# Feature projections of a Performer attention as native float32 products of 64 rows on the two halves of TensorE, with paced attention steps

## The chip, the cores and the metric

The kernel runs on one core of one Trainium2 chip. The metric is the device time of one execution in microseconds (us), as the median of several runs. A profile is one further execution, recorded by the hardware profiler. The engines are called as the profile calls them: PE is TensorE's matmul, PEld its weight load, DVE is VectorE, ACT is ScalarE, POOL is GpSimd, SP is the queue that issues the DMAs.

## The reference

A linear attention with random features is followed by two dense layers with gates, all in float32:

```python
batch, n_heads, seq, head_dim, n_features = 4, 8, 576, 64, 128
def phi(x):
    proj = np.einsum('bhsd,md->bhsm', x, omega)
    sq = np.sum(x * x, axis=-1, keepdims=True) / 2.0
    h = proj - sq
    h = h - np.max(h, axis=-1, keepdims=True)
    return np.exp(h) / np.sqrt(m)
q_p, k_p = (phi(q_s), phi(k_s))               # q_s = q * scale, k_s = k * scale
kv = np.einsum('bhsm,bhsd->bhmd', k_p, v)
num = np.einsum('bhsm,bhmd->bhsd', q_p, kv)
den = np.einsum('bhsm,bhm->bhs', q_p, k_p.sum(2))[..., None] + 1e-06
# x = (num / den) as 2304 tokens of 512, then
# layer 0: h = x @ w_in (512 -> 2048); g = h * clip(h + 3, 0, 6) / 6; x = g @ w_out
# layer 1: h = x @ w_in;               g = h * sigmoid(1.702 h);      out = g @ w_out
```

The term `sq` falls out, since the row's maximum is subtracted after it.

## The kernel before

**Tiling.** Of the 576 rows of a sequence, 512 are worked as four tiles of 128; the 64 left over of all heads go through their own tiles (`lqk`, `lv`, `el`). The work runs in blocks: the dense layers handle one batch (512 tokens) per block, 16 chunks of 128 hidden units each, layer 0 for batches 0 to 3, then layer 1 for batches 0 to 3. The last block of each layer also carries the 256 left-over tokens. The attention of batch 0 stands ahead of everything (the prologue, until 58.5 us in the profiled execution). The attention of batch n+1 is woven into block n of layer 0, so blocks 0, 1 and 2 carry attention, block 3 and layer 1 none. The first product of `emit_h` (line 439) in the blocks 1, 2, 3 and 4 starts at 183.7, 310.0, 438.8 and 570.0 us.

**Products in three parts.** A float32 product is made of three single-pass float32r products, with each operand split into a high part and a rest: hi·hi + hi·lo + lo·hi. This holds for the dense layers (`emit_h`, line 439, and `emit_o`, line 501, twelve products of 512 columns per chunk each) and for the feature projections. For these, `T` copies queries and keys of one head to float32r (`thi`, line 266) and subtracts (`tlo`, line 267), both on DVE; `TL` does the same with the left-over rows. The stationary operand of `project` (line 225) holds 64 dimensions of two row tiles in its 128 rows, and the moving operand `bd_hi`, `bd_lo` is omega twice, block by block with zeros, 256 columns. So one `PJ(h, j)` is two groups of three products of 256 columns, with j = 0 for keys and j = 1 for queries, and one bank of PSUM.

**The other steps of a head.** `features` takes the row maxima on DVE (`mx`, line 231) and four exponentials on ACT (line 233). `KV` (lines 292 and 300) multiplies feature keys with values in native float32, as pairs of products that write two halves of 64 PSUM partitions; ACT copies `kv` (line 308). `QT` (line 315) transposes the feature queries, ACT copies `qpt` (line 317). `NU` (lines 329 and 338) multiplies `qpt` with `kv`, DVE normalizes into `xt` (lines 351 to 356). `XT` (line 367) transposes a finished pair of heads, ACT and DVE split it into `x` (lines 219 and 220), which `emit_h` reads.

**Weights.** Each of the 32 chunks of weights is loaded raw and converted (`convert_w`): ACT makes `wtop` and `w` (lines 186, 187), DVE three bit operations (189 to 197), POOL two multiplications (202), DVE two additions (205), ACT casts (210), POOL subtractions (211). Layer 0's sixteen chunks are converted up to the end of block 0, layer 1's in blocks 1 to 3. Ten of the 32 half chunks of a layer stay in SBUF (`HELD`), the others are fetched again for each block.

**What sets the order.** `att_steps` lists an attention's 57 steps. In the prologue they follow one another, and the first conversion is put 12 steps before the end (`TAIL`). In a block, `side` runs one step at each of its four calls per chunk (two in `emit_h`, two in `emit_o`) until none are left. PSUM banks in a block come from four rotating buffers (`ps`), shared by `emit_h` and all attention steps. A scheduler moves instructions within each engine's list when the program is built; the lists are then fixed.

## Time and profile before

| | |
|---|---|
| runs | 984.83 us median of 3 (983.9 to 987.41) |
| profiled execution | 987.94 us, of which 986.0 us are the span |
| PE busy | 950.1 us (96%), 5626 products |
| PEld busy | 788.6 us (80%) |
| DVE busy | 470.3 us (48%) |
| ACT busy | 416.9 us (42%) |
| POOL busy | 196.3 us (20%) |
| mean granted clock of TensorE | 0.988 |

The busy time of a product includes the time in which it drains while the next one already streams, so a busy PE is not a PE at its peak. The distance between the starts of products tells what they cost. Busy shares over the whole span mix the stretch with attention and conversions (until 570 us) with the stretch of dense layers alone. The chain of waits, followed back from the last instruction, names at each step what released it.

### The profile page before, as it was taken

What the parts mean: (1) busy time and instruction counts of PE and PEld (TensorE: products, weight loads), DVE (VectorE), ACT (ScalarE), POOL (GpSimd) and SP (SyncE); (2) the same over time, 40 slices, a digit from 0 to 9 for tenths busy, and PEclk for the clock granted to TensorE, in tenths of its full rate; (3) what the DMA queues carried; (4) which work ended last, traced back from release to release, by engine and by line L of the source; (5) the groups of instructions that cost most, each with busy time, mean ns of one, the idle gap of its engine ahead of it and who ended that gap; (6) DMA issues with size and microseconds to landing.
All of it is one profiled execution on the core that took longest, in us unless ns stands there. A gap on an engine that the chain in (4) does not pass through costs nothing.

```text
span 986.0 us, 14412 instructions
## 1 busy us (share of the span) xinstructions
PE 950.1 (96%) x5626; PEld 788.6 (80%) x5626; DVE 470.3 (48%) x813; ACT 416.9 (42%) x868; POOL 196.3 (20%) x159
## 2 busy tenths in 40 slices
PE   8899999999989999999999999999999999999994
PEld 7777776888768877878888888888888888888883
DVE  7888887886776876324222232222223222322221
ACT  5876777666655664433222232132223222312221
POOL 0346565534433342021000011020002000000000
PEclk9899999999999999999999999999999999999998
DMA  6676577987787875246333374436335333422301
GB/s 197 234 262 200 199 264 251 345 298 260 269 293 260 305 249 174 74 147 214 124 121 122 126 256 149 147 130 214 128 128 192 129 128 128 137 77 86 107 1 64
DMA packets 54774, 177.22 MB, mean 180 GB/s; under 512 B 5812, under 2 KB 7476, under 8 KB 54708
## 3 DMA queue, kind: packets, MB, share of 16 engines
q1 hardware_dynamic: 54708, 176.32, 52.5%
q8 instruction: 44, 0.72, 0.3%
q14 instruction: 22, 0.18, 0.1%
HBM read 138.55 MB, written 37.75 MB: 179 GB/s over the span
## 4 chain that ended last, share of the span: by engine, by line
PE 64%; DVE 12%; DMA 7%; ACT 6%; POOL 5%; issue 3%; SPq 0%; POOLq 0%; ACTq 0%
PE ps L439 30%; PE o L501 30%; DMA ws1i<-wsn 4%; DVE w L205 4%; POOL wsn L211 3%; POOL w L202 2%; DMA ws1o<-wsn 2%; ACT wtop L186 1%; DVE gs L460 1%; DVE mx L231 1%; DVE wmag L189 1%; ACT w L187 1%; PE ps L225 1%; DVE wtop L193 1%; ACT e L233 1%
## 5 line engine op out<-in xcount | busy, mean ns | idle before, releaser
L439 PE MATMUL ps<-x,wss 128*128 128x512 f32 x1152 | 286.3, 393 | 7.7 <-ACT wss L210 6.1
L439 PEld LDWEIGHTS ps<-x,wss 128*128 128x128 f32 x1152 | 212.0, 188 | 53.0 <-ACT wss L210 7.0
L457 DVE TENSOR_TENSOR ga<-ga,ps 128x512 f32<-128x512 f32 x80 | 50.8, 635 | 252.4 <-ACT ga L456 252.4
L456 ACT ACTIVATE ga<-ps 128x512 f32<-128x512 f32 x80 | 44.4, 556 | 251.7 <-PE ps L439 251.7
L501 PE MATMUL o<-gs,wss 128*128 128x512 f32 (+1 forms) x600 | 136.8, 375 | 0.0
L460 DVE TENSOR_TENSOR gs<-ga,gs 128x512 fp32r<-128x512 f32 (+1 forms) x160 | 111.4, 712 | 47.2 <-ACT gs L459 44.2
L501 PE MATMUL o<-wss,gs 128*128 128x512 f32 x540 | 129.8, 389 | 0.0
L501 PEld LDWEIGHTS o<-wss,gs 128*128 128x128 f32 x540 | 100.7, 188 | 20.5
L501 PEld LDWEIGHTS o<-gs,wss 128*128 128x128 f32 x600 | 102.5, 189 | 17.9
L459 ACT CAST gs<-ga 128x512 fp32r<-128x512 f32 (+1 forms) x160 | 91.7, 578 | 44.1 <-DVE ga L457 32.5
L452 DVE SCALAR_TENSOR_TENSOR ga<-ga,ps 128x512 f32<-128x512 f32 x80 | 50.2, 629 | 111.2 <-ACT ga L451 111.2
L439 PE MATMUL ps<-x,wsh 128*128 128x512 f32 x384 | 95.6, 393 | 1.5 <-ACT wsh L210 0.8
L202 POOL TENSOR_TENSOR w<-w,wpow 128x512 f32<-128x512 f32 x64 | 77.3, 1229 | 94.5 <-DVE wpow L197 70.4
L451 ACT ACTIVATE ga<-ps,three 128x512 f32<-128x512 f32 x80 | 51.8, 651 | 94.9 <-PE ps L439 94.7
L501 PE MATMUL o<-gs,wsh 128*128 128x512 f32 (+1 forms) x360 | 86.1, 383 | 0.3 <-DVE gs L460 0.3
L439 PEld LDWEIGHTS ps<-x,wsh 128*128 128x128 f32 x384 | 70.9, 188 | 16.7 <-ACT wsh L210 1.3
L205 DVE TENSOR_TENSOR w<-w,wtop 128x512 f32<-128x512 f32 x64 | 73.4, 1163 | 16.8 <-POOL w L202 16.6
L501 PE MATMUL o<-wsh,gs 128*128 128x512 f32 x324 | 78.5, 389 | 0.0
L541 POOL TENSOR_TENSOR x<-xr,x 128x512 fp32r<-128x512 f32 x16 | 22.2, 1417 | 263.8 <-ACT x L540 263.8
L233 ACT ACTIVATE e<-ps,mx 128x128 f32<-128x128 f32 x220 | 63.7, 387 | 25.3 <-DVE mx L231 25.2
L501 PEld LDWEIGHTS o<-gs,wsh 128*128 128x128 f32 x360 | 64.1, 195 | 12.6 <-DVE gs L460 0.7
L501 PEld LDWEIGHTS o<-wsh,gs 128*128 128x128 f32 x324 | 60.4, 188 | 12.3
(123 smaller groups left out, 1003.8 us busy)
## 6 DMA issues: line engine op xcount, KB each, us to landing
wss<-ws1i SPq DMA_DIRECT2D x48, 512.0 KB, 3.2
wss<-ws1o SPq DMA_DIRECT2D x40, 512.0 KB, 3.3
wss<-ws0i SPq DMA_DIRECT2D x36, 512.0 KB, 4.4
wraw<-in_w_in_dram SPq DMA_DIRECT2D x32, 512.0 KB, 4.5
wraw<-in_w_out_dram SPq DMA_DIRECT2D x32, 512.0 KB, 6.0
wss<-ws0o SPq DMA_DIRECT2D x30, 512.0 KB, 3.5
ws1i<-wsn SPq DMA_DIRECT2D x16, 512.0 KB, 3.8
ws1o<-wsn SPq DMA_DIRECT2D x16, 512.0 KB, 2.9
```

Of the source, the lines that this page charges most:

```text
L202: nc.gpsimd.tensor_tensor(out=w[:, cols], in0=w[:, cols], in1=q[:, cols], op=ALU.mult)
L205: nc.vector.tensor_tensor(out=wj, in0=wj, in1=a[:, j * DM:(j + 1) * DM], op=ALU.add)
L211: nc.gpsimd.tensor_tensor(out=s[:, 1], in0=wj, in1=s[:, 0].bitcast(F32), op=ALU.subtract)
L233: act = nc.scalar.activation(out=e[:, r, :], in_=ps[:, r, :], func=AF.Exp, bias=mx[:, r:r + 1])
L439: nc.tensor.matmul(out=ps, lhsT=w[:, wi, kk, :], rhs=x[:, xi, kk, :], start=(m == 0), stop=(m == 3 * NK - 1),)
L451: nc.scalar.activation(out=g, in_=ps, func=AF.Relu, bias=three)
L452: nc.vector.scalar_tensor_tensor(out=g, in0=g, scalar=6.0, in1=ps, op0=ALU.min, op1=ALU.mult)
L456: nc.scalar.activation(out=g, in_=ps, func=AF.Sigmoid, scale=1.702)
L457: nc.vector.tensor_tensor(out=g, in0=g, in1=ps, op=ALU.mult)
L459: nc.scalar.copy(s[:, 0, :], g)
L460: nc.vector.tensor_tensor(out=s[:, 1, :], in0=g, in1=s[:, 0, :].bitcast(F32), op=ALU.subtract)
L501: last = nc.tensor.matmul(out=ps[:, e, :], lhsT=lhsT, rhs=rhs, start=(c == 0 and m == 0 and per == 1), stop=(c == NC - 1 and m == 2 and e ...
```

## The change

The split of keys, queries and left-over rows is gone, with `T`, `TL`, `bd_hi` and `bd_lo`. `project` is one native float32 product per row tile: 64 rows of the raw `qk` tile are stationary, the 128 columns of `omt` (omega times the scale) are moving. The two row tiles that shared a stationary operand before now use the lower and the upper 64 rows of the array, each with a PSUM bank of its own. `PJ(h)` covers keys and queries in one step, eight products, `PL` the left-over rows, eight products. The feature tile `e` holds keys and queries, with three buffers (`EB`). `KV` comes ahead of `QT`. The steps are 39, and `side` runs one only when the share of steps done falls behind the share of its 64 calls in a block. `HELD` goes from 10 to 11, `TAIL` from 12 to 10.

```diff
-    def project(ps, lhs_hi, lhs_lo):
-        o = ps.rearrange("p a m -> p (a m)")
-        for n, (a, w) in enumerate(((lhs_hi, bd_hi), (lhs_hi, bd_lo), (lhs_lo, bd_hi))):
-            nc.tensor.matmul(
-                out=o, lhsT=a, rhs=w.rearrange("p a m -> p (a m)"), start=(n == 0), stop=(n == 2)
-            )
+    HALVES = (slice(0, D), slice(D, 2 * D))
+
+    def project(ps, n, rows, lhsT):
+        nc.tensor.matmul(out=ps[:, n, :], lhsT=lhsT, rhs=omt[rows, :], start=True, stop=True)
...
-        def T(self, h):
...
-        def PJ(self, h, j):
-            hi, lo = self.t[h]
-            ps = bank([P, R, M], "ps")
-            for g in range(2):
-                project(ps[:, 2 * g:2 * g + 2, :], hi[:, j, g, :], lo[:, j, g, :])
-            e = at.tile([P, R, M], F32, tag=f"e{j}", bufs=2, name="e")
-            self.feat[h] = features(ps, e)
-            self.e[h, j] = e
+        def PJ(self, h):
             a = qkv[self.b, h // 2][0][:, h % 2]
+            ps = [bank([P, R, M], "ps") for _ in HALVES]
+            for j in range(2):
+                for g in range(2):
+                    for p, rows in zip(ps, HALVES):
+                        project(p, 2 * j + g, rows, a[rows, j, g, :])
+            e = at.tile([P, 2, 2, 2, M], F32, tag="e", bufs=EB, name="e")
+            for half, p in enumerate(ps):
+                self.feat[h] = features(p, e[:, half].rearrange("p j g m -> p (j g) m"))
+            self.e[h] = e
...
             if 1 <= h <= H:
+                st.append(lambda h=h: a.KV(h - 1))
                 st.append(lambda h=h: a.QT(h - 1))
-                st.append(lambda h=h: a.KV(h - 1))
...
+    pace = [0, 0]
 
     def side():
-        if todo:
+        pace[1] += 1
+        while todo and (pace[0] - len(todo)) * 4 * NC < pace[0] * pace[1]:
             todo.pop()()
```

**The projections on PE.** In the list of PE, batch 0's fourth head stood before as six products of 256 columns for the keys, with the queries' six after other work (the names are output and inputs):

```order
L225 MATMUL ps_389<-bd_hi_85,thi_332 128x256
L225 MATMUL ps_389<-bd_lo_86,thi_332 128x256
L225 MATMUL ps_389<-bd_hi_85,tlo_333 128x256
L225 MATMUL ps_389<-bd_hi_85,thi_332 128x256
L225 MATMUL ps_389<-bd_lo_86,thi_332 128x256
L225 MATMUL ps_389<-bd_hi_85,tlo_333 128x256
L329 MATMUL acc_345<-kv_302,qpt_289 64x65 x8
```

Now the same head's first products alternate between two banks, one for each half of the rows:

```order
L302 MATMUL acc_322<-ident_78,e_230 128x128 x4
L226 MATMUL ps_339<-omt_143,qk_154 128x128
L226 MATMUL acc_340<-omt_143,qk_154 128x128
L226 MATMUL ps_339<-omt_143,qk_154 128x128
L226 MATMUL acc_340<-omt_143,qk_154 128x128
```

Not every set of eight stands like this. Batch 0's fifth head has the four products of one half together, then a transposition `XT` (line 354 now), then the four of the other half:

```order
L302 MATMUL ps_396<-ident_78,e_273 128x128 x4
L226 MATMUL ps_410<-omt_143,qk_329 128x128 x4
L354 MATMUL acc_403<-ident_78,xt_294 128x128 x4
L226 MATMUL acc_411<-omt_143,qk_329 128x128 x4
L279 MATMUL acc_448<-v_155,e_349 64x65
L316 MATMUL ps_434<-kv_394,qpt_401 64x65 x8
```

Over the whole list, 23 of the 36 sets of eight products alternate (some of these with one neighbour out of place), in 6 the two halves follow as four and four, and in 7 other work stands between the two halves.

**Steps apart.** In block 1 before, between `NU` (lines 329 and 338) and the `XT` that transposes its result (line 367), PE had this:

```order
L329 MATMUL ps<-kv,qpt 64x65 x8
L338 MATMUL ps<-kv,qtl 64x65 x2
L439 MATMUL ps<-x_864,wsh 128x512 x6
L315 MATMUL ps<-ident,e 128x128 x4
L439 MATMUL ps<-x_864,wsh 128x512 x6
L292 MATMUL ps<-v,e 64x65 x8
L300 MATMUL ps<-lv,el 64x65 x2
L367 MATMUL ps<-ident,xt 128x128 x4
```

Now, at one such place in block 1 (`NU` is lines 316 and 325, `KV` 279 and 287, `QT` 302, `XT` 354, the dense layers 421 and 483):

```order
L316 MATMUL ps<-kv,qpt 64x65 x8
L325 MATMUL ps<-kv,qtl 64x65 x2
L421 MATMUL ps<-x_774,wss 128x512 x12
L279 MATMUL ps<-v,e 64x65 x8
L287 MATMUL ps<-lv,el 64x65 x2
L483 MATMUL o<-gs,wsh 128x512 x6
L302 MATMUL ps<-ident,e 128x128 x4
L483 MATMUL o<-gs,wsh 128x512 x6
L421 MATMUL ps<-x_774,wss 128x512 x6
L354 MATMUL ps<-ident,xt 128x128 x4
```

The dense products between the two steps went from 12 to 30.

**ACT at the first conversion.** In the prologue, ACT's list had the first conversion (lines 186 and 187) between the features of the fifth head and the copy of `kv`:

```order
L317 COPY qpt_521<-acc_516 128x512
L233 ACTIVATE e_490<-acc_483,mx_491 128x128 x4
L186 ACTIVATE wtop_695<-wraw_383 128x1024
L187 ACTIVATE w_698<-wraw_383 128x1024
L187 ACTIVATE w_871<-wraw_386 128x1024
L308 COPY kv_534<-ps_523 128x65
```

Now the same three stand there, ahead of `kv` and `qpt` (lines 295 and 304):

```order
L232 ACTIVATE e_420<-acc_411,mx_427 128x128 x4
L187 ACTIVATE wtop_632<-wraw_333 128x1024
L188 ACTIVATE w_635<-wraw_333 128x1024
L188 ACTIVATE w_781<-wraw_336 128x1024
L295 COPY kv_459<-acc_448 128x65
L304 COPY qpt_466<-ps_461 128x512
```

Here the place of the conversion stayed; the order of `kv` and `qpt` behind it is turned round.

## Rows read from the trace of the kernel before

**Rows 1.** The page, busy time, share of the span and instructions of each engine.

```profile
PE 950.1 (96%) x5626; PEld 788.6 (80%) x5626; DVE 470.3 (48%) x813; ACT 416.9 (42%) x868; POOL 196.3 (20%) x159
```

**Rows 2.** Busy time by stretch: prologue and blocks 0, 1, 2.

```profile
core 0: us, PE busy (x) PEld busy (x) DVE busy (x) ACT busy (x) POOL busy (x), PEclk, DMA share, GB/s
0.00:58.50 58.50, 49.55 (x511) 42.24 (x511) 46.04 (x110) 40.89 (x115) 14.78 (x19) 0.94 0.70 229
58.50:183.70 125.20, 118.95 (x807) 93.36 (x807) 106.29 (x173) 88.29 (x172) 72.30 (x56) 1.00 0.71 246
183.70:310.00 126.30, 122.91 (x841) 99.30 (x840) 93.62 (x160) 78.78 (x167) 50.12 (x39) 0.99 0.79 279
310.00:438.80 128.80, 125.67 (x854) 101.68 (x853) 75.52 (x131) 67.96 (x156) 34.04 (x28) 0.99 0.57 196
```

**Rows 3.** Chain of waits, shares of the stretch 0 to 184 us by line.

```profile
by line: DVE w L205 13.8%; POOL w L202 6.8%; PE ps L439 5.7%; DVE mx L231 5.5%; DVE wmag L189 5.4%; issue 5.1%; ACT wtop L186 4.8%; DVE gs L460 4.6%; DVE wtop L193 4.3%; ACT e L233 3.7%; PE ps L225 3.1%; DVE tlo L267 2.7%; DVE thi L266 2.5%
```

**Rows 4.** PE timeline, dense layers alone: start, us, engine, line, op, out<-in, shape, count.

```profile
640.97 2.88 PE L501 MATMUL o<-wss,gs 128*128 128x512 f32 x12
643.69 2.88 PE L439 MATMUL ps<-x,wss 128*128 128x512 f32 x12
```

**Rows 5.** PE timeline in block 2: dense products, KV and a projection's first products.

```profile
403.53 1.52 PE L439 MATMUL ps<-x,wss 128*128 128x512 f32 x6
404.98 0.69 PE L292 MATMUL ps<-v,e 128*64 128x65 f32 x16
405.60 0.33 PE L300 MATMUL ps<-lv,el 64*64 64x65 f32 x4
405.86 1.66 PE L439 MATMUL ps<-x,wss 128*128 128x512 f32 x6
407.36 0.28 PE L225 MATMUL ps<-bd_hi,thi 128*128 128x256 f32 x1
407.48 0.28 PE L225 MATMUL ps<-bd_lo,thi 128*128 128x256 f32 x1
```

**Rows 6.** PE timeline: products with 64 rows and all 128 columns of the array.

```profile
58.46 0.46 PE L374 MATMUL acc<-ident,xln 64*128 64x64 f32 x4
58.86 3.93 PE L439 MATMUL ps<-x,wss 128*128 128x512 f32 x16
```

**Rows 7.** PE timeline: NU's left-over products and KV's first ones.

```profile
22.11 0.34 PE L338 MATMUL ps<-kv,qtl 128*64 128x65 f32 x3
22.23 0.27 PE L292 MATMUL ps<-v,e 128*64 128x65 f32 x1
22.28 0.22 PE L338 MATMUL ps<-kv,qtl 128*64 128x65 f32 x1
```

**Rows 8.** Operand splits, grouped by line: busy us, mean ns, then idle before.

```profile
L267 DVE TENSOR_TENSOR tlo<-qk,thi 128x512 fp32r<-128x512 f32 x32 | 24.5, 765 | 0.1
L266 DVE CAST thi<-qk 128x512 fp32r<-128x512 f32 x32 | 18.4, 575 | 11.0 <-PE ps L225 6.5 <-DMA qk<-in_qk_dram 2.7 <-PE acc L225 1.8
```

**Rows 9.** PE timeline: four of its waits, in brackets idle us and releaser.

```profile
31.54 1.13 PE L329 MATMUL acc<-kv,qpt 128*64 128x65 f32 x16 [2.43 <-ACT kv L308]
56.66 0.73 PE L439 MATMUL ps<-x,wss 128*128 128x512 f32 x2 [2.21 <-ACT wss L210]
286.20 0.63 PE L367 MATMUL ps<-ident,xt 128*128 128x128 f32 x4 [2.57 <-DVE xln L356]
375.08 0.69 PE L292 MATMUL ps<-v,e 128*64 128x65 f32 x16 [2.24 <-DVE tlo L267]
```

**Rows 10.** Granted clock after two waits (columns as rows 2), and dense products there.

```profile
287.40:290.50 3.10, 3.10 (x9) 2.36 (x8) 1.61 (x3) 1.42 (x4) 1.28 (x1) 0.50 0.55 169
376.20:379.30 3.10, 3.10 (x8) 2.43 (x9) 1.99 (x4) 1.03 (x3) 1.29 (x1) 0.50 0.51 155
287.14 4.50 PE L501 MATMUL o<-gs,wsh 128*128 128x512 f32 x12
```

**Rows 11.** ACT timeline in the prologue: conversions, then the copy of `kv`.

```profile
29.18 2.20 ACT L187 ACTIVATE w<-wraw 128x1024 f32<-128x1024 uint32 x2
31.23 0.26 ACT L308 COPY kv<-ps 128x65 f32<-128x65 f32 x1
```

More of the change, by code (lines that the diff above doesn't have):

```diff
@@ L78, in performer_moe_kernel @@
     LAG = 2
-    TAIL = 12
+    EB = 3
+    TAIL = 10
     WARM = 8
     FIRST = 4
-    HELD = 10
+    HELD = 11
     AHEAD = 2
@@ L636, in performer_moe_kernel @@
                 todo = steps[::-1]
+                pace[:] = len(todo), 0
             if (l, n, c) == (0, B - 2, NC - 1):
                 while todo:
-                    side()
+                    todo.pop()()
                 actx.close()
@@ L660, in performer_moe_kernel @@
                 while todo:
-                    side()
+                    todo.pop()()
         if u >= LAG:
```

70 lines of the change are left out of this document (20 added, 50 removed).

## The prediction

> **What bounds the kernel now.** I read the busy times first, then the stretches, the chain and the waits of PE. PE is busy for 96% of the span and no other engine for half of it [rows 1], but this busy time contains the drain of each product. In the dense layers alone, twelve products of 512 columns start 2.72 us ahead of the next twelve, so one costs 0.227 us [rows 4]. With such spacings I added up PE's own work in a block that carries attention: 384 dense products (87.0 us); nine projections of twelve products, each 0.118 us by the starts 407.36 and 407.48 [rows 5] (12.7); `KV` eight times 0.88 [rows 5] (7.0); `NU`, products of the same form, about 6.0; 52 transpositions at about 0.118 (6.1). PE also pays when the shape of the array changes: six dense products ahead of `KV` take 1.45 us and the six behind it 1.50 [rows 5], where 6 × 0.227 is 1.36, so 0.09 going in and 0.14 coming out. 17 such excursions make 3.9. Together that is 122.7 us, of which 35.7 are attention. Blocks 1 and 2 last 126.3 and 128.8 us [rows 2], so PE waits for some 9.7 us in them. The prologue and block 0 hold two attentions and one block of dense work, 158.4 us, and last 183.7 [rows 2]: 25 us of waits. Afterwards there is next to nothing to win: PE streams dense products. So the kernel is PE's own work plus about 35 us of waits, nearly all before 440 us.
>
> What the waits are for: in the first 184 us the chain runs through DVE above all, with the additions and bit operations of the conversions, and the operand splits `tlo` and `thi` have 2.7% and 2.5% of it [rows 3]. Single waits of PE are for a `kv` copy behind conversions on ACT, for a converted weight, for a normalization, and, at 375.08, for DVE's `tlo` [rows 9]. After the two waits in blocks 1 and 2 the granted clock is 0.50, that is 1.2 GHz, for about 3 us; twelve dense products from 287.14 on take 4.50 us less a drain, where 2.72 is usual [rows 10].
>
> **The change part by part.** My account is in differences against the profiled execution, 987.94 us with 986.0 in the span. It lies 0.3% above the median of 984.83, and I put the same difference on the median.
>
> *Projections on PE.* Before: 36 sets (32 heads, four left-over ones) of 12 products at 0.118 make 51.0 us. After: 36 sets of eight products. The trace shows native float32 in `KV`: eight products appear as 16 instructions [rows 5], so each is two. Such a pair of instructions, one in each half of the columns, is done in 0.62/8 = 0.078 us for 65 columns; this includes a first weight load. Scaled to 128 columns this is at most 0.153. The other end is 0.059, if 128 columns cost half of what 256 columns of float32r do. I take 0.118: the projection before also loads 128 weight columns per product, and 65 columns at 0.078 less one load give nearly the same. For the range I keep 0.11 to 0.13 and give the ends small weight.
>
> Whether two halves of the *rows* run side by side is not in the trace; two halves of the columns do [rows 5]. The Trainium skill, page TensorEngine Tiling (Array Packing), section Key Properties, says that different tiles can load weights and multiply in parallel; no run here shows it for row halves. I take them as parallel where the list alternates (23 sets, eight slots) and as serial where it doesn't (13 sets, 16 slots): 23 × 8 × 0.118 + 13 × 16 × 0.118 = 21.7 + 24.5 = 46.2 us. So 4.8 are won on the products. If all were serial it would be 36 × 16 × 0.118 = 68.0, if all were parallel 34.0.
>
> PE need not keep to the list: an instruction of `KV` starts at 22.23, ahead of the last one of `NU` at 22.28 that stands before it in the list [rows 7]. The Trainium skill, page TensorE: Matmul & The Clock Gate, Part 3 (The mechanism), calls matmuls strictly first in, first out; this row differs, and the measurement decides. By the row, the six sets of four and four would overlap by some three slots each, 2 us in all; by the rule, by none. I leave these 2 us to the range.
>
> *Shape changes.* A projection before had the dense layers' shape; now it has 64 rows. Along PE's list the shape changes 181 times before and 231 times now. Entering and leaving cost 0.09 + 0.14 around `KV`. For 64 rows the nearest row has four small products take 0.40 us [rows 6], of which their columns explain some 0.2, so a load of 0.2 comes on top of the entry. So a change is worth 0.12 to 0.19 us; I take the upper, 50 × 0.19 = 9.5, since the new shape is that of the last row. PE's own work so goes from 51.0 to 46.2 + 9.5: **+4.7 us**.
>
> *Operand splits on DVE.* `thi` and `tlo` go, 18.4 + 24.5 = 42.9 us of DVE [rows 8], and with them those of the left-over rows. DVE is busy for 46 of 58.5 us in the prologue and 106 of 125 in block 0 [rows 2]. What this is worth is their part of the chain, 5.2% of 184 = 9.6 us at most, and 0 at least, should ACT take their place: it is busy for 41 of 58.5 us there, and the first conversion still stands ahead of the `kv` copy in ACT's list, so that 2.20 us of conversion [rows 11] and the wait of 2.43 behind them [rows 9] stay. I take two thirds: **−6 us**.
>
> *Blocks 1 and 2.* Two waits stand out, 2.57 us of `XT` for a normalization and 2.24 of `KV` behind `tlo` [rows 9]. Each brings the low clock, at about 1.8 us [rows 10]: 8.4 of the 9.7 us. The second has a split as its releaser. In the first, `XT` comes 12 dense products after `NU`; in the paced list it comes 30 after it, 18 × 0.227 = 4.1 us later, more than the wait. What is late next is the row maximum behind a weight addition on DVE, and PSUM: a projection now fills two of the four banks at once and drains them one after the other. I take **−7 us**, between 0 and −9.7.
>
> *At nothing:* the third feature buffer (exponentials wait for maxima, not for `e`); one more held half chunk (DMA is busy for at most 0.79 in any of these stretches [rows 2], and PE's waits don't name a fetch); `KV` ahead of `QT`, which swaps two copies on ACT. The pacing adds no wait of its own: a step is only issued later, and the dense products stand in between. At the end of a block the last `XT` comes one or two products' groups before the next block reads it; ACT and DVE have to split in that time, behind whatever is queued. If that cover fails, it is a wait like those of 2.5 us above, three times.
>
> Sum: 4.7 − 6 − 7 = −8.3 us: 979.6 on the profiled execution, **976 us** on the median.
>
> **The rivals.** *The row halves run one after the other.* Then PE's work rises by 68.0 + 9.5 − 51.0 = 26.5 us. It decides from about 13 us on, since that is what the waits give back: 984.8 + 26.5 − 13 = 998 us, slower. For it: no row shows row halves in parallel. Against it: column halves run in parallel, and the two halves here write different banks.
>
> *The waits move and don't shrink.* ACT and the conversions set the pace of the first 184 us, the pressure on four banks that of blocks 1 and 2. Then only the 4.7 us remain: 989 to 990 us. For it: ACT's list is unchanged at the first conversion, and POOL and ACT have a large part of the chain [rows 3]. Against it: a split is named as a releaser.
>
> *PE overlaps the halves in all sets, and all the waits named go.* 34.0 + 9.5 − 51.0 = −7.5, with −13: 964 us. For it: PE starts ahead of its list [rows 7]. Against it: there it jumped over three instructions, here it would have to jump over eight, and in seven sets other work stands between.
>
> **How the numbers follow.** Forecast 0.55 (968 to 984), serial halves 0.13, waits that stay 0.20, full overlap 0.12. The range from 964 to 996 leaves out the far end of the serial case and of the overlap and takes in 0.11 to 0.13 us per slot (±4 us) and both ends of the waits. A measurement of this kernel can tell about 0.5% (4.9 us) from no change. Faster by more: most of the forecast, and the full overlap, 0.60. Within: the rest of the forecast and most of the waits that stay, 0.21. Slower: the serial halves and the rest, 0.19.
>
> **What would show it.** The starts of an alternating set: pairs a few ns apart and about 0.12 us from pair to pair, so that eight products take about 0.95 us; if it is 1.9, the halves are serial. Sets of four and four: near 1.9. The dense products around a set: 0.1 to 0.4 us more. In the stretches: the prologue and block 0 together near 180 us, blocks 1 and 2 near 124 and 125, blocks from 570 us on unchanged. The granted clock should stay at 2.4 GHz between 200 and 440 us. No wait of PE should name a maximum's bank for more than 1 us. The prediction is wrong if the first 184 us don't get shorter, or if a shape change with 64 rows costs well over 0.2 us.

## The result and the profile after

The changed kernel takes 993.2 us (median; 991.64 to 995.32) where the kernel before takes 984.37 beside it: a ratio of 1.0086, 95% interval 1.0064 to 1.0107. It is 0.86% slower; the forecast was 976 us. The profiled executions are only 3.7 us apart, 991.64 and 987.94, since the one of before is a long one of its kernel and the one of after a short one. So the traces can explain 3.7 us of the 8.8 us between the medians; the other 5.1 us lie between executions and stand in neither trace.

The page of after, in answer to [rows 1], and the same four stretches as in [rows 2] (us, then busy time and instructions of each engine, granted clock, DMA share, GB/s):

```profile
PE 955.4 (97%) x5770; PEld 782.7 (79%) x5770; DVE 437.8 (44%) x733; ACT 415.9 (42%) x868; POOL 193.8 (20%) x159
```

```profile
0.00:58.50 58.50, 46.77 (x514) 38.30 (x514) 37.37 (x75) 42.26 (x113) 20.35 (x23) 0.82 0.71 240
58.50:183.70 125.20, 121.28 (x838) 94.31 (x839) 102.49 (x162) 89.27 (x178) 69.86 (x55) 0.97 0.70 242
183.70:310.00 126.30, 121.73 (x869) 94.72 (x867) 89.27 (x141) 80.55 (x169) 54.63 (x43) 1.00 0.80 289
310.00:438.80 128.80, 128.68 (x916) 100.67 (x915) 59.36 (x114) 60.96 (x144) 20.91 (x16) 1.00 0.49 167
```

DVE has lost 32 us of work in all, but only 12.5 us in the first 184 us (46.04 + 106.29 before, 37.37 + 102.49 now), although 18 heads' splits are gone from there: other work has moved in. POOL shows it: 20.35 us in the first stretch instead of 14.78. The granted clock fell to 0.82 in the first stretch and stayed at 1.00 behind 184 us.

The blocks' first dense products start at 40.7, 183.7, 310.0, 438.8 and 570.0 us before, and at 43.7, 192.0, 318.3, 445.3 and 573.9 after. From here on these starts are the marks between the stretches, and "prologue" means the time up to the first of them, although the last heads of batch 0 come behind it. The marks shift a little with the order: by the traces, 192 products of the second layer (`emit_o`) stand ahead of block 1's first product after, and 180 before, and 12 products take 2.7 us. So about 5.6 of the 8.3 us at 192.0 are a loss. Block 2 gives some 2 us of it back. What block 3 gives back, 2.6 us, is the shift alone.

Batch 0's attention itself is over much later. Its last transposition of a pair of heads starts here, before and after:

```profile
57.93 0.60 PE L367 MATMUL acc<-ident,xt 128*128 128x128 f32 x4
```

```profile
67.29 0.65 PE L354 MATMUL acc<-ident,xt 128*128 128x128 f32 x4
```

What PE waits for in the first part, before (0 to 190 us) and after (0 to 200 us), the rows that the argument uses; columns: engine, tile, line, releaser, us in total, times, longest:

```profile
PE ps L439 <- ACT wss L210: 6.1, 4, 2.2
PE acc L329 <- ACT kv L308: 2.4, 1, 2.4
PE ps L329 <- ACT kv L308: 1.1, 2, 0.6
PE ps L439 <- ACT wsh L210: 0.8, 1, 0.8
PE ps L439 <- POOL wss L211: 0.7, 1, 0.7
PE ps L439 <- POOL wsh L211: 0.6, 1, 0.6
```

```profile
PE acc L316 <- ACT qpt L304: 2.8, 1, 2.8
PE ps L226 <- ACT e L232: 2.7, 2, 1.6
PE ps L354 <- DVE den L338: 2.5, 2, 1.9
PE ps L421 <- DVE ga L434: 2.2, 1, 2.2
PE acc L354 <- DVE den L338: 1.5, 1, 1.5
PE ps L287 <- ACT el L232: 1.5, 1, 1.5
```

Before, 8.2 us of these waits are for converted weights (`wss`, `wsh`). After, no wait for a weight is left, and attention waits instead: for exponentials (`e`, `el`), for the copy `qpt`, for normalizations (`den`). In blocks 1 and 2 the waits of [rows 9] at 286.20 and 375.08 have no successor; what stands there now (200 to 570 us of after) is small:

```profile
PE ps L421 <- ACT e L232: 1.0, 1, 1.0
PE ps L226 <- DVE ga L434: 0.9, 1, 0.9
PE ps L279 <- ACT e L232: 0.6, 2, 0.4
```

To set own work against waits I took from the records, for each pair of neighbouring operations on PE, the usual distance of their starts (the 20th percentile over all traces of this study). What goes beyond it by more than 0.25 us counts as a wait; dense products at 0.38 to 0.45 us count the difference to 0.227 as low clock; the rest is PE's own. Up to block 4 (570.0 us before, 573.9 after) this gives, in us:

| | own work | waits and low clock: to block 1 | in block 1 | in block 2 |
|---|---|---|---|---|
| before | 543.5 | 14.5 | 5.4 | 5.1 |
| after | 547.6 | 20.8 | 4.1 | 0.0 |

Own work rose by 4.1. Waits fell by 6.4 in blocks 1 and 2 and rose by 6.3 ahead of them. (Low clock on attention's small products is not separated; it stays in own work. The table's stretches end with the next block's first dense product, whose place in the order differs between kernels, so I compare waits by stretch and own work in the sum only. And where two operations are neighbours in one or two places only, a wait there passes for their usual distance and counts as own work: 3.0 us for `den` in the first run below, and 3.3 us for `qpt` in the two runs with a chain.)

### The profile page after: what moved, and what is told of

The parts are those of the page before. It is cut to its first block, busy times and chain, and to the rows that moved or that the text cites. A ratio compares the mean times of both kernels' runs of the same rounds, so it can differ in the third digit from the quotient of the medians.

```text
span 989.9 us, 14600 instructions
## 1 busy us (share of the span) xinstructions
PE 955.4 (97%) x5770; PEld 782.7 (79%) x5770; DVE 437.8 (44%) x733; ACT 415.9 (42%) x868; POOL 193.8 (20%) x159
## 4 chain that ended last, share of the span: by engine, by line
PE 70%; DVE 9%; ACT 7%; POOL 5%; DMA 4%; issue 2%; POOLq 0%; ACTq 0%; DVEq 0%
PE ps L421 33%; PE o L483 32%; DMA ws1i<-wsn 4%; DVE w L206 3%; POOL w L203 3%; PE ps L226 2%; POOL wsn L212 2%; ACT wtop L187 2%; ACT e L232 2%; DVE wmag L190 1%; DVE wtop L194 1%; ACT wss L211 1%; DVE mx L230 1%; ACT w L188 1%; DVE wpow L198 1%
## 5 line engine op out<-in xcount | busy, mean ns | idle before, releaser
L421 PE MATMUL ps<-x,wss 128*128 128x512 f32 x1056 | 263.9, 396 | 1.7 <-ACT e L232 1.0
L421 PEld LDWEIGHTS ps<-x,wss 128*128 128x128 f32 x1056 | 195.9, 189 | 43.6 <-ACT e L232 1.3
L483 PE MATMUL o<-gs,wss 128*128 128x512 f32 (+1 forms) x600 | 139.5, 376 | 0.0
L421 PE MATMUL ps<-x,wsh 128*128 128x512 f32 x480 | 120.4, 398 | 2.9 <-DVE ga L434 2.2
L421 PEld LDWEIGHTS ps<-x,wsh 128*128 128x128 f32 x480 | 89.6, 190 | 22.5 <-DVE ga L434 2.4
L203 POOL TENSOR_TENSOR w<-w,wpow 128x512 f32<-128x512 f32 x64 | 74.1, 1178 | 83.3 <-DVE wpow L198 52.9
L206 DVE TENSOR_TENSOR w<-w,wtop 128x512 f32<-128x512 f32 x64 | 82.0, 1298 | 17.3 <-POOL w L203 17.1
L483 PE MATMUL o<-gs,wsh 128*128 128x512 f32 (+1 forms) x360 | 83.2, 376 | 0.6 <-DVE gs L442 0.3
L232 ACT ACTIVATE e<-ps,mx 128x128 f32<-128x128 f32 x224 | 62.9, 383 | 20.8 <-DVE mx L230 20.7
L483 PEld LDWEIGHTS o<-gs,wsh 128*128 128x128 f32 x360 | 61.4, 189 | 12.6 <-DVE gs L442 0.7
L483 PEld LDWEIGHTS o<-wsh,gs 128*128 128x128 f32 x324 | 60.4, 188 | 12.3
```

What stands on the lines that cost most here:

```text
L203: nc.gpsimd.tensor_tensor(out=w[:, cols], in0=w[:, cols], in1=q[:, cols], op=ALU.mult)
L206: nc.vector.tensor_tensor(out=wj, in0=wj, in1=a[:, j * DM:(j + 1) * DM], op=ALU.add)
L232: act = nc.scalar.activation(out=e[:, r, :], in_=ps[:, r, :], func=AF.Exp, bias=mx[:, r:r + 1])
L421: nc.tensor.matmul(out=ps, lhsT=w[:, wi, kk, :], rhs=x[:, xi, kk, :], start=(m == 0), stop=(m == 3 * NK - 1),)
L483: last = nc.tensor.matmul(out=ps[:, e, :], lhsT=lhsT, rhs=rhs, start=(c == 0 and m == 0 and per == 1), stop=(c == NC - 1 and m == 2 and e ...
```

## The experiments

In the expectations of four runs (pacing alone, no pacing, conversions held, half of the splits left out), theory A says that the conversions, freed of the splits on DVE, moved ahead of attention in the lists of ACT and DVE; rival B, that the products of 64 rows leave PE idle enough for the low clock; rival C, that the pacing costs. Ratios are to the kernel before on the same chip, with the 95% interval. "Waits" are those of the table above, low clock included: first up to block 1, then the sum.

### The pacing

Pacing alone on the kernel before, and the changed kernel without it:

```
 def side():
-    if todo:
+    pace[1] += 1
+    while todo and (pace[0] - len(todo)) * 4 * NC < pace[0] * pace[1]:
         todo.pop()()
```

> The kernel before with one part of the change alone: the attention steps paced over a block (57 steps over 64 calls); products, splits, buffers as before. Theory A (in the changed kernel the weight conversions, freed of DVE's splits, moved ahead of the attention in the lists of ACT and DVE and made the prologue longer): pacing has no part in the first 58 us, so the second emit_h starts at 52 us as before, and only blocks 1 and 2 can win up to 5 us: 979 to 985. Rival C (the pacing costs the first 190 us): block 1 starts 4 to 8 us later than 183.7, 988 to 992.

Measured: 993.72 us, 1.0091 (1.0065 to 1.0116). Waits 23.1 to block 1 and 27.8 in all. Its waits in block 0 (39 to 199 us):

```profile
PE ps L439 <- ACT wss L210: 8.1, 6, 2.2
PE o L501 <- ACT gs L459: 5.7, 3, 3.4
PE ps L367 <- DVE den L351: 3.0, 1, 3.0
```

The waits for weights do not shrink (11.1 us in all, 8.2 before), since the conversions set the pace of block 0 there, and paced attention steps no longer stand in them: they come behind the last chunk and wait for normalizations and `gs`. Block 1 starts at 198.2 us instead of 183.7, of which 2.7 us are 12 dense products more ahead of the mark. That is rival C, somewhat over its range.

> The changed kernel with one step at every call as before instead of the pacing. Theory A: the prologue stays as in the changed kernel (second emit_h at 62 us, block 1 at 190 to 194), and blocks 1 to 3 lose what the pacing gave them, 2 to 5 us: 994 to 998. Rival C: block 1 starts at 184 to 187, 985 to 989.

Measured: 1003.56 us, 1.019 (1.0172 to 1.0209). Without the pacing the changed kernel loses 10 us more, which neither expectation had. Own work is 550.5, 2.9 more, and the waits are 32.4. In the trace, 25 rows of four products of one half stand alone instead of 13; what that costs is measured below.

Pacing in blocks 1 and 2 alone, on the kernel before (`pace[2]` is the number of the block, and the lines stand ahead of the paced loop):

```
+    if pace[2] == 0:
+        if todo:
+            todo.pop()()
+        return
```

> The kernel before with the pacing alone, and that only in blocks 1 and 2; block 0 issues its steps as before. With pacing in all blocks the blocks 0 to 3 took 159.0, 126.7, 123.8 and 128.7 us, without it 143.0, 126.3, 128.8 and 131.2. If pacing costs in block 0, where the weights are being converted, and wins behind it: 5 to 8 us less than the kernel before, 0.992 to 0.995. If what it won in blocks 1 and 2 was only handed on from block 0: within 2 us of the kernel before, 0.998 to 1.002. If pacing costs everywhere: over 1.003.

Measured: 982.28 us, 0.998 (0.9968 to 0.9992). The waits of blocks 1 and 2 fall from 10.5 to 3.6, which is what the prediction expected of them; only about 2 us of it reach the time. So pacing costs in block 0 and wins behind it, less than forecast.

### The place of the conversions

```
-                convert_next(c + 2)
+                convert_next(c + 2, *(att.feat[7] if c < 4 else ()))
```

> The changed kernel with the conversions of the second and the next chunks of weights held behind the features of batch 0's last head, so that they stand later in the lists of ACT and DVE. Theory A: the second emit_h starts at 52 to 56 us instead of 62.5, the clock is at 1.2 GHz for less than 15 us before 192 instead of 27, block 1 starts at 183 to 187: 984 to 989. Rival B (the native products of 64 rows themselves leave PE so idle that the clock falls): waits and clock stay, 990 to 996. If weights now come late, the waits turn into waits of emit_h for weights and the time is as it was, 991 to 995.

Measured: 994.44 us, 1.01 (1.0078 to 1.0122): no gain. The held chunks are 1 to 4 (`c < 4`), one fewer than the expectations further below say. The lists did change as meant. This is how long the split of a chunk's first half (the half chunk for `emit_h`) ends on POOL ahead of the first dense product with it, in us, from the records (the last row is from the last run of this section):

| chunk | 1 | 3 | 5 | 7 | 9 | 11 | 13 | 15 |
|---|---|---|---|---|---|---|---|---|
| before | 3.6 | -0.4 | -1.4 | -1.0 | -0.6 | 0.3 | 0.3 | 2.3 |
| after | 21.2 | 18.4 | 17.7 | 14.5 | 13.2 | 15.3 | 15.9 | 12.9 |
| after, conversions held | 0.4 | -0.1 | -1.5 | 0.9 | 1.0 | 2.6 | -0.2 | -1.6 |
| held, block 0 not paced | 0.4 | 0.9 | 5.1 | 8.1 | 10.1 | 15.6 | 4.6 | 0.0 |
| the same, chunk 1 left free | 13.6 | 11.3 | 11.7 | 15.2 | 21.5 | 26.5 | 17.6 | 8.1 |

(A product with the high parts can start before the low parts are there, hence the small negative numbers.) One pair of rows from after shows the lead of chunk 11: POOL is done with it at 129.18 + 1.29 = 130.5, of which `wsh`, the half chunk for the first layer of products, at 129.2; the products start at 144.53 and wait for DVE, not for the weight:

```profile
127.59 1.62 POOL L212 TENSOR_TENSOR wsh<-w,wsh 128x512 fp32r<-128x512 f32 x1 [1.28 <-ACT wsh L211]
129.18 1.29 POOL L212 TENSOR_TENSOR wss<-w,wss 128x512 fp32r<-128x512 f32 x1
```

```profile
144.53 2.04 PE L421 MATMUL ps<-x,wsh 128*128 128x512 f32 x5 [2.22 <-DVE ga L434]
```

So the conversions do run 13 to 21 us ahead of their use in the changed kernel. With them held, batch 0's last transposition comes at 57.9 us instead of 67.3, as in the kernel before:

```profile
57.94 0.65 PE L354 MATMUL acc<-ident,xt 128*128 128x128 f32 x4
```

The fifth chunk's products start at 80.6 us instead of 88.4 (before: 80.3), but the weights are again just in time, and waits up to block 1 are 25.1 instead of 20.8. That looked like the paced block 0 of the first run. So both were undone together, the second time with chunk 1 left free (`0 < c < 4`):

> The changed kernel with the conversions of chunks 1 to 5 held behind the features of the last head, as in the run before that gained nothing, and with block 0 not paced. Theory A: two effects lengthen the first 190 us of the changed kernel and hide the relief of VectorE. Conversions run 10 to 22 us ahead of their use and stand in front of the first attention; and where they are held, a paced block 0 leaves attention steps for behind its last chunk (16.8 us from the last chunk to the end of the block in that run, 3.8 in the kernel before), while earlier each chunk waits for its weights. Both undone: block 0 ends near 183 instead of 195.4, 979 to 985 us in all, 0.994 to 1.000 of the kernel before. Rival B (the native products cost what they cost, wherever the steps stand): no better than the changed kernel, 1.006 to 1.011. Rival C (unpaced, heads' halves stand apart again and cost 1.5 us each): 1.000 to 1.006.

Measured: 988.62 us, 1.0036 (1.0021 to 1.0051), outside the changed kernel's interval. Block 0 ends at 179.3 us instead of 192.0, and the waits up to block 1 are 12.8, less than the 14.5 of before. Three of its stretches (prologue, block 0, block 1) and its waits in block 1:

```profile
0.00:42.20 42.20, 36.30 (x397) 29.97 (x397) 20.47 (x47) 26.98 (x84) 5.86 (x11) 0.80 0.64 215
42.20:179.30 137.10, 132.12 (x983) 102.33 (x982) 110.90 (x185) 100.92 (x202) 77.59 (x61) 1.00 0.70 235
179.30:315.70 136.40, 129.90 (x901) 101.29 (x899) 95.40 (x149) 82.44 (x170) 59.55 (x45) 0.99 0.81 287
```

```profile
PE ps L421 <- DVE ga L434: 5.6, 2, 3.2
PE ps L226 <- DVE ga L434: 0.5, 1, 0.5
```

Block 1 then takes 136.4 us instead of 126.3. Part of that is a mere shift of dense products across the mark: 168 products of the second layer stand ahead of block 1's first product here, 192 in the changed kernel and 180 in the kernel before, so 5.4 of the 12.7 us by which block 0 ends sooner are order (2.7 of the 4.4 us against the kernel before). That also holds for the 16.8 and 3.8 us that I set against each other in the expectation: 24 products, some 5 us of their difference, are order and no loss. The other part is new waits of 5.6 us for DVE. What is left of the gain is 2.7 us of waits in all (22.2 instead of 24.9) in the trace and half a per cent in the time. Rival B falls: with the same native products the clock of block 0 is 1.00.

> The same, but only the conversions of chunks 2 to 5 are held, so that chunk 1 starts its conversion near 33 us instead of 44.4 and the whole row of conversions runs some 5 to 8 us earlier. Theory A: block 0 ends 2 to 6 us before that of the other run, 975 to 983 us in all, 0.990 to 0.998 of the kernel before, if TensorE's own work (170 us to the end of block 0) is not yet the bound. Rival B: as the changed kernel, 1.006 to 1.011. If chunk 1's conversion again stands in front of the first attention: slower than the other run by 3 us or more.

Measured: 989.91 us, 1.0052 (1.0033 to 1.0071), the same as the run before it within the intervals. Waits 17.9 up to block 1. The earlier start of the conversions brings nothing, so they are no longer the bound. And a long lead does no harm by itself: the leads are as long here as in the changed kernel, or longer, but batch 0's last transposition comes at 59.6 us. What the held conversions give back is their place in front of the last heads of batch 0.

### What VectorE's relief is worth

On the kernel before, the second half of each split is left out; the products take the high part in its place:

```
-            self.split_in(hi, lo, a)
-            self.t[h] = (hi, lo)
+            nc.vector.tensor_copy(hi, a)
+            self.t[h] = (hi, hi)
```

> The kernel before without the rests of queries and keys: the subtraction on DVE is left out and the third product takes the high part again, so PE's work is unchanged and 25 us of DVE work are gone; the result is less exact. Theory A: conversions move ahead of the attention here too, the second emit_h starts at 56 to 62 us and block 1 at 186 to 191: 986 to 991. My prediction's own step (less DVE work shortens the first 184 us): 977 to 981. Rival B (the products' shape) says nothing of a loss here: 977 to 985.

Measured: 980.11 us, 0.9957 (0.9943 to 0.9971). Block 1 begins at 180.3 us instead of 183.7, and the wait for `tlo` in block 2 is gone: waits 18.2 instead of 25.0, 4.6 of the difference in block 2. In the kernel before, somewhat more than half of the split work is worth 3.4 us ahead of block 1, so 6 us for all of it was of the right size there.

The other way round, splits that no one reads were put back into the changed kernel, first right ahead of a head's products, then a head ahead:

```
         def PJ(self, h):
             a = qkv[self.b, h // 2][0][:, h % 2]
+            hi = at.tile([P, 2, 2, P], F32R, tag="thi", bufs=1, name="thi")
+            lo = at.tile([P, 2, 2, P], F32R, tag="tlo", bufs=1, name="tlo")
+            nc.vector.tensor_copy(hi, a)
+            nc.vector.tensor_tensor(out=lo, in0=a, in1=hi.bitcast(F32), op=ALU.subtract)
```

> The changed kernel, in which VectorE splits the keys and queries of each head as before, although no one reads the result: 43 us of VectorE work put back. If the term of the prediction was right in the changed kernel too (their removal is worth 6 us, and something else ate it): 4 to 8 us slower than the changed kernel, 1.013 to 1.017 of the kernel before. If VectorE's relief is worth nothing in the changed kernel, since ACT, POOL and the normalizations set its waits: within 2 us of it, 1.006 to 1.011.

Measured: 1020.64 us, 1.0367 (1.034 to 1.0393), far over either expectation.

> As the run with VectorE's unread splits, but each head's splits come a head ahead, behind the maxima of the head before, where the kernel before had them. If it was the place right ahead of the maxima that cost 27 us: 4 to 10 us slower than the changed kernel, 1.013 to 1.019 of the kernel before, and the prologue near 45 us instead of 55. If VectorE's 43 us themselves cost that: 1.03 or more. If the splits had been hidden: 1.006 to 1.011.

Measured: 1018.85 us, 1.0351 (1.0324 to 1.0379). The place of the splits is not the cause. But DVE itself waits in this run, here in its first 190 us, and 12.6 us of it ahead of the first dense product, which comes 13.3 us later than in the changed kernel:

```profile
DVE thi L264 <- DMA qk<-in_qk_dram: 15.0, 6, 5.8
DVE w L206 <- POOL w L203: 8.2, 11, 1.3
```

In the kernel before that wait is 2.7 us [rows 8]. There, by the program, the split frees a buffer of keys and queries as soon as DVE has read it; in these runs it is free only when PE has multiplied from it too, and the load of the fourth pair of heads is issued at 24.2 us, where the kernel before has it at 16.4 and the changed kernel at 18.2. That this is what delays the loads was not tested. These two runs therefore measure more than DVE's work. The third gives DVE the same two instructions on a tile that is always there:

> The changed kernel with the same two VectorE instructions for each head, but on a tile that is always there, so that they never wait for a load (in the runs with the unread splits VectorE stood still for 14 and 15 us behind loads of keys and queries). If the removal of the splits is worth about what the prediction took, 6 us, also in the changed kernel: 4 to 9 us slower than it, 1.013 to 1.018. If the 25 us of those runs were VectorE's work and not the loads: 1.03 or more. If VectorE's relief is worth nothing: 1.006 to 1.011.

Measured: 1013.68 us, 1.0299 (1.0267 to 1.0331), 21 us more than the changed kernel. Nearly all of it is in the prologue, which ends at 61.7 us instead of 43.7:

```profile
0.00:61.70 61.70, 41.62 (x397) 34.16 (x397) 57.65 (x116) 31.73 (x90) 10.81 (x15) 0.76 0.49 164
```

```profile
PE ps L365 <- DVE den L349: 7.3, 1, 7.3
PE acc L365 <- DVE den L349: 5.0, 1, 5.0
```

DVE is busy for 57.65 of 61.70 us, and PE waits 12.3 us for normalizations. But this is not DVE's old load. Nothing ties these instructions to their heads, and all 32 pairs, those of the later batches too, stand in the prologue, 39.2 us of work. Ahead of its first dense product the kernel before has nine heads' splits, 10.0 us, and the left-over rows' 1.1. This run and the kernel before, by line:

```profile
L265 DVE TENSOR_TENSOR thi<-load,thi 128x512 fp32r<-128x512 f32 x32 | 23.9, 746 | 0.5
L264 DVE CAST thi<-load 128x512 fp32r<-128x512 f32 x32 | 15.3, 478 | 0.5
```

```profile
L267 DVE TENSOR_TENSOR tlo<-qk,thi 128x512 fp32r<-128x512 f32 x9 | 6.2, 685 | 0.1
L266 DVE CAST thi<-qk 128x512 fp32r<-128x512 f32 x9 | 3.8, 424 | 5.8 <-DMA qk<-in_qk_dram 2.7 <-PE acc L225 1.8 <-PE ps L225 1.2
```

So none of the three runs puts the old load back as it was: two wait for loads, and the third moves the work of four batches into the first. What DVE's relief is worth in the changed kernel is not shown. The run does not contradict the 6 us.

### Groups that do not alternate

Each product of a group was tied behind the one before it, and the half whose bank comes free last goes first:

```
+        with behind(prev):
+            return nc.tensor.matmul(
+                out=ps[:, n, :], lhsT=lhsT, rhs=omt[rows, :], start=True, stop=True
+            )
...
-                    for p, rows in zip(ps, HALVES):
-                        project(p, 2 * j + g, rows, a[rows, j, g, :])
+                    for p, rows in zip(ps[::-1], HALVES[::-1]):
+                        last = project(p, 2 * j + g, rows, a[rows, j, g, :], last)
```

> The changed kernel with its row-half products tied into a chain, so that the two halves alternate in TensorE's list also where they stood four and four. Theory A (TensorE's own work grew because 13 of 41 groups do not alternate): in the traces so far an alternating head with its surroundings costs 1.43 us, four and four in one piece 1.86, and four and four with dense products between them 2 x 1.45. Five or six heads of the last kind and six of the second give 5 to 10 us, less about 0.4 us for each head whose first product now stands alone: 4 to 7 us less than the changed kernel, 1.002 to 1.005 of the kernel before. Rival B (the scheduler's other choices, and waits, decide): no change, 1.007 to 1.011. Rival C (the chain makes TensorE wait for two banks at once): slower than the changed kernel, over 1.012.

Measured: 999.08 us, 1.014 (1.0113 to 1.0166). Theory A is right on PE's own work, 541.7 instead of 547.6 us, 5.9 less (and 3.3 us more, if the wait for `qpt` from the remark under the table is taken out of it). Rival C is right on the time: the waits rise from 24.9 to 40.5, for `qpt`, `ga` and exponentials, which fits a group that can start only when both banks are free (that link was not tested by itself):

```profile
PE acc L321 <- ACT qpt L309: 6.9, 4, 3.3
PE ps L227 <- DVE ga L439: 4.7, 1, 4.7
PE ps L227 <- ACT e L235: 3.0, 1, 3.0
```

> The changed kernel, in which the row halves are chained to alternate in the first attention alone. With the chain everywhere the first dense product started at 37.9 us instead of 43.7, and blocks 0 and 1 lost 13.5 us in waits. If the gain in the prologue is the chain's own and the waits come from chaining beside the dense layers: 4 to 6 us less than the changed kernel, 1.002 to 1.005. If a prologue that is done sooner only meets the weights' conversion later: within 2 us of the changed kernel, 1.006 to 1.011. If the order of the blocks behind it falls out worse by chance: over 1.012.

Measured: 993.0 us, 1.0095 (1.0071 to 1.0118): as the changed kernel. The first dense product starts at 38.2 us instead of 43.7, and the next two blocks give it back: block 1 starts at 189.9 us instead of 192.0, block 2 at 318.5 instead of 318.3.

### Buffers, held chunks, and two banks at once

Two features buffers, alone (`EB = 2`) and together with ten held half chunks (`EB = 2`, `HELD = 10`):

> The changed kernel with two features buffers in place of three; every engine's list stays exactly as it is. If the third buffer is worth nothing, as the prediction had it: within 2 us of the changed kernel, 1.006 to 1.011, and the 12 us that two buffers and ten held half chunks cost together come from the held half chunk, which changes all the lists. If exponentials wait for the second buffer: 1.015 or more.

Measured: 994.02 us, 1.0104 (1.0083 to 1.0126). The third buffer is worth nothing that can be measured.

> The changed kernel with two features buffers and ten held half chunks, as before. The prediction put both at nothing: within 2 us of the changed kernel, 1.006 to 1.011 of the kernel before. If the third buffer is what lets the exponentials of a head run ahead: 3 us slower or more, over 1.012. If the eleventh held chunk and the third buffer only disturb the order: faster, below 1.005.

Measured: 1005.16 us, 1.021 (1.0178 to 1.0241), waits 37.2. So beside two buffers the eleventh held half chunk is worth about 11 us, and not by its fetch: no wait of PE in this trace names one. All lists come out in another order. Its counterpart on the kernel before (`HELD = 9`):

> The kernel before with nine held half chunks instead of ten: no instruction of an engine's own work is added or taken away but the fetch of one half chunk in each block, yet all lists are planned anew. If such an edit is neutral: 0.998 to 1.002. If each list of this kernel is as good as its order happens to come out, and the order of the kernel before was a good one: 3 to 10 us slower, 1.003 to 1.010. A gain, below 0.997, would mean that the order of the kernel before was an ordinary one.

Measured: 981.19 us, 0.9976 (0.9958 to 0.9993). It is a little faster; the order of the kernel before was not a lucky one.

The exponentials of the keys ahead of those of the queries, and, in the kernel before, both banks filled ahead of both maxima and the eight exponentials:

```
+            for j in range(2):
+                for half, p in enumerate(ps):
+                    for g in range(2):
+                        r = 2 * j + g
+                        act = nc.scalar.activation(
+                            out=e[:, half, j, g, :], in_=p[:, r, :], func=AF.Exp,
+                            bias=mx[half][:, r:r + 1],
+                        )
```

> The changed kernel, in which ScalarE takes the exponentials of a head's keys (half of each bank) before those of its queries; same instructions, another order. In the kernel before, a head's keys fill one bank and its queries another, so its keys are done after one maximum and four exponentials; in the changed kernel each bank holds half of both, and the products of keys and values need all eight. If that coupling makes the first 190 us longer: 3 to 6 us less than the changed kernel, 1.003 to 1.006 of the kernel before, the first dense product near 40 us instead of 43.7. If not: 1.006 to 1.011.

Measured: 997.19 us, 1.0122 (1.0095 to 1.0148). No gain.

> The kernel before with its projections as they are, but with the features of a head taken as the changed kernel takes them: both banks are filled first, then come both maxima, then the eight exponentials in turn from either bank. If the coupling of the two banks is what the first 190 us lose in the changed kernel: they grow by 5 to 12 us, 1.004 to 1.012 of the kernel before. If not: within 3 us of it, 0.997 to 1.003.

Measured: 982.78 us, 0.9976 (0.9959 to 0.9992). Taking the features of both banks at once costs nothing in the kernel before. This theory falls by both runs.

Last, the two small gains on the kernel before together (`HELD = 9`, pacing in blocks 1 and 2):

> The kernel before with pacing in blocks 1 and 2 alone and nine held half chunks: the two edits that each came out faster, by 0.2% and 0.24%. If they add up: 0.994 to 0.997. If both take away the same waits of blocks 1 and 2: 0.997 to 0.999. If the order falls out worse: over 1.0.

Measured: 981.55 us, 0.9963 (0.9949 to 0.9977), with waits of 18.2. It beats the kernel before by a third of a per cent and has none of the native products. Whether the two gains add up is not shown, since its interval overlaps those of either edit alone. No order tried with the native products came below 1.0036.

## Why the prediction was wrong

*Projections and shape changes: the sum was right, +4.7 predicted and +4.1 measured, the parts less so.* By the distances of the table, the projections themselves won about 2 us (4.8 predicted), and the dense products lost about 6 (9.5 predicted for the shape changes). Both parts were taken too large, so that the sum fits is partly luck. Row halves do run side by side: in an alternating group the two starts of a pair are 6 to 7 ns apart and the pairs about 0.112 us. Three groups of after, each with the next dense product behind it: an alternating one, one of four and four in one piece, and one half alone (start, us, line, count):

```profile
381.54 1.16 PE L226 MATMUL ps<-omt,qk 64*128 64x128 f32 x16
382.64 0.97 PE L421 MATMUL ps<-x,wsh 128*128 128x512 f32 x3
```

```profile
368.10 1.71 PE L226 MATMUL ps<-omt,qk 64*128 64x128 f32 x16
369.74 0.96 PE L421 MATMUL ps<-x,wss 128*128 128x512 f32 x3
```

```profile
319.93 1.16 PE L226 MATMUL ps<-omt,qk 64*128 64x128 f32 x8
321.02 0.96 PE L421 MATMUL ps<-x,wss 128*128 128x512 f32 x3
```

They take 1.10, 1.64 and 1.09 us. Four and four in one piece overlap by about three slots (two halves one after the other would be some 2 us), as I had left open. The Trainium skill, page TensorEngine Tiling (Array Packing), section Key Properties, has tiles multiply in parallel, and this trace agrees for row halves; its page TensorE: Matmul & The Clock Gate, Part 3 (The mechanism), has products go strictly in order, and the 1.64 us differ from that. Between dense products an alternating head costs 1.31 us more than these alone, a half alone 1.31 as well, and four and four 1.86; in the kernel before a head cost twice 0.72. (The 1.43 and 1.45 in an expectation above contain the entry into the next group.) So the group whose halves stand apart costs double, and the pacing, by making them rarer, earned 2.9 us.

*Blocks 1 and 2: right, -7 predicted and -6.4 measured.* Both waits that I named are gone, and the clock is 1.00 from 184 to 439 us. By the run with the pacing in these blocks alone, it is the pacing that removes them: without the native products it takes the waits from 10.5 to 3.6. Leaving out the second half of the splits removes the second of the two waits as well.

*The first 184 us: the step that failed.* The term "operand splits on DVE, -6 us" took the lists around the splits to stay as they were. In the kernel before the term holds in size (3.4 us in this stretch for somewhat more than half of the split work). In the changed kernel waits up to block 1 grew by 6.3 us, 12 us from the term, and that is the whole miss that the traces show: -8.3 + 12 is their 3.7 us. The runs show two things that I had not costed. The conversions moved up into the room that the splits left, in front of the last heads of batch 0, whose attention ends 9.4 us later and waits for DVE and ACT; and a paced block 0 leaves attention steps for its end. With both undone the waits up to block 1 are 12.8, which is 8.0 of the 12 us. This stretch then ends at 179.3 us, 4.4 ahead of before, but 2.7 of that is order, so the gain is 1.7 us and not 6. And the kernel as a whole gains only half a per cent by the two edits: other waits for DVE follow in block 1. So small a gain could come from lists planned anew, which alone moved the time by 0.2 to 1%; what speaks for the conversions is that batch 0's last transposition came back to 57.9, 58.6 and 59.6 us in all three runs that held them.

*"At nothing."* Right for the third buffer. Wrong for the held half chunk, at 11 us, and for "the pacing adds no wait of its own", at 8.6 us or more of waits up to block 1 on the kernel before. The buffers of keys and queries, which PE now holds longer, were not in the sum at all; in the changed kernel no wait of PE names their load.

*The rivals.* What happened is the second, "the waits move and don't shrink": 25.0 us of waits before, 24.9 after, and PE's own work on top. It gave 989 to 990 us on the median, and 987.94 + 4.7 on the profiled execution is 992.6, where 991.64 was measured. But its reason was another one: it had the conversions keep their place in an unchanged list of ACT, and had the waits of each stretch stay. In the runs the conversions moved, the waits of blocks 1 and 2 went, and as much came on top in the first stretch; that the sum stayed is luck. A split as the releaser of one wait weighed too much against this rival, which had a chance of 0.20. Serial halves and the full overlap did not occur.

*What stays open.* What DVE's relief is worth in the changed kernel, since no run puts back the old load alone. Where the other 4 of the 12 us come from: coupled banks, the order of exponentials, the third buffer and the groups that don't alternate were tried, and none of these edits made the kernel faster. Why the gain of the first stretch comes back as waits for DVE in block 1. And 5.1 of the 8.8 us between the medians lie in no trace.

## What to carry to other kernels

Where several in-order engines are near their limits in turn, work taken from one of them is a gain only if what moves into its place is not ahead of something that is needed sooner: look at what then stands in front of it in each engine's list, and hold that back. A long lead of a producer over its consumer is a hint to look there, not a loss by itself. Work put back to test a term has to be tied to where it stood, or the scheduler moves it, as it did with the 39.2 us here. Spreading steps evenly helps where the engine that they interrupt is the bound, and costs where they filled waits for something else. Edits that add no work but let the lists be planned anew moved this kernel by 0.2 to 1%, so a forecast of 1% from summed terms needs the new lists, and not only the new terms.

## What the runs showed of the hardware

VectorE's additions of two tiles in SBUF can take more than twice as long beside GpSimd. All additions of the weights, and the maxima, of after (duration in ns, min/median/max):

```profile
L206 DVE TENSOR_TENSOR w<-w,wtop x64: 674/1626/1779, 29.4 to 348.0; 128x512 f32<-128x512 f32 x64
```

```profile
L230 DVE TENSOR_REDUCE mx<-ps x63: 672/679/693, 6.3 to 410.9; 128x4 f32<-128x512 f32 x63
```

By the records, the 13 additions with GpSimd idle (5% of their time at most) take 678 ns on average, and the 10 with GpSimd busy for 90% or more 1537, one of them 678; the maxima, which read PSUM, take 679 with it and without it. The Trainium skill, page SBUF — State Buffer, section SBUF: two separate sides, says that a VectorE instruction with two inputs in SBUF and a GpSimd instruction that reads SBUF take turns on one pair of ports; the trace agrees, 678 against 1537 ns. So conversions that run early on GpSimd can also delay VectorE's part of attention; no run here separates that.

The granted clock was at 1.2 GHz for longer in the prologue of after than in that of before, from 29.2 to 42.5 us (before: 31.4 to 38.0), although PE shows 11.36 us of busy time in these 13.3; in block 0 of after it fell three times behind waits of 1.1 to 2.2 us. The stretch in the prologue and the last of the three:

```profile
29.20:42.50 13.30, 11.36 (x90) 9.45 (x90) 10.82 (x20) 10.68 (x26) 8.91 (x8) 0.50 0.79 278
145.20:148.40 3.20, 3.20 (x9) 2.53 (x8) 2.68 (x4) 1.66 (x2) 1.92 (x2) 0.50 0.43 169
```

The run with both effects undone has the same clock in its prologue, 0.80, and the shorter first stretch all the same. So the prologue's clock is not what makes the two differ; whether it costs in both was not tried. In its block 0 the clock does not fall, where after has the three stretches of some 3 us: these go with the waits.
